# Idle products in w1, a narrower last block of w2, one product for each layer norm sum, and six chunks of V on VectorE in three groups

## The chip, the cores and the metric

The kernel runs on one core of one Trainium2 chip. The metric is the device time of one execution in microseconds (us). Where this text names engines it uses the profile's short names: PE is the matrix engine (TensorE), PEld its weight loads, DVE is VectorE, ACT is ScalarE, POOL is GpSimd, and SP is the engine whose queue issues the loads.

## The reference

One token goes through two identical pairs of layers: an attention with a long cache, and a dense layer with gelu. Everything is float32.

```
D = 512; H, Sk, Dh = 32, 4096, 128; F = 1376
def A(x):                      # 32 heads, one query
    q = (x @ wq) per head
    p = softmax(q . k_cache * Dh**-0.5)
    return (p . v_cache) @ wo
def B(x):
    return gelu(x @ w1 + b1) @ w2 + b2
x = A_x
x = x + A(layernorm(x)); x = x + B(layernorm(x))
x = x + A(layernorm(x)); x = x + B(layernorm(x))
```

The two passes use the same caches and the same weights. K and V are 67 MB each, so the work is nearly all reading.

## The kernel before, in words

The 32 heads are worked in 8 groups of 4. A group's K and its V are one block each of 128 rows by 16384 columns (8.4 MB), cut into C = 8 chunks of NC = 2048 columns. Three homes in one large tile, `arena`, hold blocks in turn (`RING`). A pair of weight blocks (a group's wo and the next group's wq, 2 MB) has a home of its own, `PAIR`. All these loads are issued on SP's one queue, in the order of the program, as soon as the place they write to has been read for the last time. In a steady group SP issues pair, K, V in a row: the pair's home is free once `out_product` of the group before has run, K's and V's homes are free by then too.

A group runs like this. `group` first adds the last partial sums of the group before (`sum_up`, 4 products on PE), then computes the scores of its K (32 products of 8 by 512), then `out_product` of the group before, then the softmax. `partly` works on V: PE takes the first BY_PE = 3 chunks (`values`), and `weighted` lets DVE multiply the other 5 chunks by their weights in place (line 266) and add them up pairwise (line 271). Meanwhile `next_queries` on PE makes the queries of the next group. `sum_up` waits for DVE's last addition.

The first pass goes through groups 0 to 7, the second through 7 to 0; in the second the loop variable `n` counts from 2 to 7, and n = 2 to 6 work as above. Between the passes stands the first `mlp`. It has no spare home: each of its 11 blocks of w2 (512 columns each) is loaded over the four rows of w1, so `load_w2(c)` is issued as soon as the products with row c of w1 have run, and the loads of the next weights and of K (`behind_w2`) are issued as soon as blocks of w2 have been used. At the end, the second `mlp` has w1 and w2 in homes of their own, loaded in pieces far ahead.

`mlp` computes x @ w1 in 4 steps of 4 products (one for each quarter of the F columns, FJ = 344 columns each), and beside it the layer norm's mean and variance: `minus_mean` makes a sum over 128 partitions with four products of 32 columns of weights each. The hidden vector is turned into 32 by 11 blocks, 4 quarters below each other; 11 times 32 is 352, so each quarter is padded by 8 rows on the host. Then come 11 steps of 4 products with w2.

`idle` issues a product of zeros with something that already lies in `arena`; its result is used by nobody. Each float32 product stands as two rows on PE and two on PEld in the profile.

## Time and profile before

| what | value |
|---|---|
| time, median of 3 runs | 673.58 us (673.3 to 674.3) |
| profiled execution, its own time | 673.92 us |
| its span, first to last instruction | 672.1 us |
| mean granted TensorE clock | 0.782 |
| PE, DVE, ACT, POOL busy | 59%, 49%, 3%, 1% |
| moved by the DMA queues | 285.98 MB, 425 GB/s over the span |

The page gives busy times by engine, the span in 40 slices, and the groups of instructions. Busy shares of a whole span mix stages; so the trace is asked by stretch. A releaser behind an arrow is what ended an idle time. "In flight" on the chain of waits, a DMA row, is the time from the issue of a load to its landing, so it holds the time in which the load stood behind others in its queue.

### The profile page before, as it was taken

The page shows a single profiled execution, that of the slowest core. Times are in us where ns is not written, and L with a number is a line of the kernel's source. Part 1 is how long each engine was busy: PE and PEld are TensorE (multiplying, and loading weights), DVE is VectorE, ACT ScalarE, POOL GpSimd, SP SyncE. Part 2 cuts the span into 40 slices and gives each one's busy share as a digit, 9 for nine tenths or more (in the row PEclk, how much of TensorE's full clock was granted, in tenths as well). Part 3 has the DMA queues.
Part 4 walks back from the last instruction along what each step waited for, and adds up shares of the span by engine and source line. Part 5 has one row for each costly group of instructions (what it writes and reads, how often), then busy time and mean ns, then how long its engine had stood idle before and what let it go on. Part 6 is the DMA issues. An engine that isn't in the chain of part 4 may idle for free. (4 is left out here: it accounts for less than half of the span.)

```text
span 672.1 us, 5775 instructions
## 1 busy us (share of the span) xinstructions
PE 397.9 (59%) x2460; PEld 108.2 (16%) x2460; DVE 329.1 (49%) x480; ACT 22.8 (3%) x48; POOL 4.8 (1%) x23
## 2 busy tenths in 40 slices
PE   3442753747617556386777878738526566284685
PEld 1110210211102111121213222101101112021122
DVE  2049186293682845912212221492772936918522
ACT  0010000000000000002000110000000000000000
POOL 1000000000000000000000000000000000000000
PEclk9567775887758757777978999987759767688788
DMA  9999999999999999999999999999999999999996
GB/s 375 437 437 434 437 430 437 410 461 437 437 434 404 462 430 414 433 438 422 435 413 384 432 451 425 427 445 434 430 429 416 458 433 433 434 433 414 433 418 275
DMA packets 11545, 285.98 MB, mean 425 GB/s; under 512 B 1792, under 2 KB 1792, under 8 KB 3584
## 3 DMA queue, kind: packets, MB, share of 16 engines
q1 hardware_dynamic: 11088, 285.61, 98.9%
q8 instruction: 19, 0.31, 0.2%
q10 hardware_dynamic: 432, 0.01, 0.0%
q14 instruction: 6, 0.05, 0.0%
HBM read 285.62 MB, written 0.00 MB: 425 GB/s over the span
## 5 line engine op out<-in xcount | busy, mean ns | idle before, releaser
L111 PE MATMUL pO<-arena,cells 128*128 128x512 f32 (+4 forms) x376 | 93.7, 632 | 147.2 <-DVE arena L271 128.2
L111 PE MATMUL pS<-arena,front 128*8 128x512 f32 x1036 | 145.5, 702 | 36.2 <-DMA arena<-in_k 32.4
L266 DVE TENSOR_TENSOR arena<-arena 128x10240 f32<-128x10240 f32 x11 | 119.1, 10825 | 31.6 <-DMA arena<-in_v 28.2
L111 PE MATMUL pO<-arena 128*4 128x512 f32 x584 | 94.5, 804 | 44.5 <-DMA arena<-in_v 42.7
L271 DVE TENSOR_TENSOR arena<-arena 128x2048 f32<-128x2048 f32 (+1 forms) x33 | 98.5, 2984 | 0.7
L229 DVE TENSOR_REDUCE cells<-pS 128x1 f32<-128x512 f32 x16 | 11.1, 692 | 154.3 <-PE pS L111 154.3
L111 PEld LDWEIGHTS pO<-arena,cells 128*128 128x128 f32 (+3 forms) x376 | 27.9, 122 | 197.3 <-DVE arena L271 137.4
L111 PEld LDWEIGHTS pS<-arena,front 128*8 128x8 f32 x1036 | 31.3, 101 | 157.0 <-issue 116.1
L111 PE MATMUL pS<-arena,cells 128*1 128x128 f32 (+1 forms) x328 | 49.2, 362 | 6.8 <-DMA arena<-in_w 4.6
L281 DVE STREAM_TRANSPOSE arena<-pO 128x512 f32<-128x512 f32 x16 | 11.5, 717 | 55.0 <-PE pO L111 55.0
L243 PE MATMUL pO<-front,arena 128*128 128x128 f32 x64 | 13.1, 339 | 36.6 <-ACT arena L238 36.6
L111 PEld LDWEIGHTS pO<-arena 128*4 128x4 f32 x584 | 16.5, 102 | 108.3 <-issue 103.3
L238 ACT ACTIVATE arena<-pS,cells 128x512 f32<-128x512 f32 x16 | 12.4, 778 | 500.4 <-DVE cells L234 500.4
L170 DVE STREAM_TRANSPOSE arena<-pO 32x128 f32<-32x128 f32 x64 | 19.9, 311 | 18.3 <-PE pO L111 17.3
L111 PEld LDWEIGHTS pS<-arena,cells 128*1 128x1 f32 (+1 forms) x328 | 21.5, 113 | 42.1 <-issue 32.5
L232 DVE TENSOR_REDUCE cells<-cells 128x1 f32<-128x8 f32 x16 | 2.6, 161 | 29.4 <-PE pO L111 29.2
L243 PEld LDWEIGHTS pO<-front,arena 128*128 128x128 f32 x64 | 8.2, 163 | 49.6 <-ACT arena L238 48.4
L170 DVE STREAM_TRANSPOSE arena<-pS 32x128 f32<-32x128 f32 x44 | 13.7, 310 | 0.8
L248 DVE STREAM_TRANSPOSE cells<-cells 128x32 f32<-128x32 f32 x16 | 3.4, 214 | 6.7 <-ACT arena L238 5.5
L172 DVE STREAM_TRANSPOSE arena<-pS 128x128 f32<-128x128 f32 x3 | 0.9, 317 | 10.3 <-PE pS L111 10.3
L383 DVE MEMSET pS<- 128x512 f32 x11 | 5.3, 485 | 1.2
L198 DVE TENSOR_SCALAR cells<-cells,pS 128x4 f32<-128x4 f32 x4 | 0.9, 234 | 9.0 <-PE pS L111 9.0
(63 smaller groups left out, 74.6 us busy)
## 6 DMA issues: line engine op xcount, KB each, us to landing
arena<-in_w SPq DMA_DIRECT2D x13, 2048.0 KB, 11.3
arena<-in_k SPq DMA_DIRECT2D x4, 4096.0 KB, 25.0
arena<-in_v SPq DMA_DIRECT2D x2, 4096.0 KB, 38.8
arena<-in_w SPq DMA_DIRECT2D x6, 1024.0 KB, 20.5
arena<-in_v SPq DMA_DIRECT2D x3, 2048.0 KB, 42.7
arena<-in_v SPq DMA_DIRECT2D x1, 6144.0 KB, 30.3
arena<-in_w SPq DMA_DIRECT2D x6, 688.0 KB, 31.2
arena<-in_v SPq DMA_DIRECT2D x4, 1024.0 KB, 46.5
```

The lines of the kernel that those rows point to most:

```text
L111: tc.keep_in_program_order(nc.tensor.matmul(*a, **kw))
L170: nc.vector.transpose(t[q], src[q, P * j : P * (j + 1)])
L172: nc.vector.transpose(t, src[:, :P])
L229: nc.vector.tensor_reduce(ml[:, 0:1], pS, axis=AX.X, op=ALU.max)
L232: nc.vector.tensor_reduce(m, mt[:, :C], axis=AX.X, op=ALU.max)
L238: nc.scalar.activation(p, pS, AF.Exp, bias=bias[:, 0:1], scale=sc, accum_out=ml[:, 0:1])
L243: tc.keep_in_program_order(nc.tensor.transpose(pT[:, b].rearrange("p j r -> p (j r)"), p[:, P * b : P * (b + 1)], ident))
L248: nc.vector.transpose(lt, ml)
L266: nc.vector.tensor_tensor(t, t, w.unsqueeze(2).to_broadcast([P, 4 * J * (C - BY_PE), P]), op=ALU.mult)
L271: nc.vector.tensor_tensor(a, a, b, op=ALU.add)
L281: nc.vector.transpose(ot, pO)
L383: nc.vector.memset(pS, 0.0)
```

## The change

Four parts.

1. **Idle products in w1.** In the first `mlp` three idle products are put behind the first three steps of w1, of 128, 256 and 256 columns, after that step's `load_w2`. They write columns 128 and up of the PSUM tile `pS`.
2. **w2's last block of 96 rows.** FJ becomes 352 and the four quarters of F are no longer padded each: three have 352 columns and the last has 320 (`FL`). So w2's 11th block has only 96 rows that matter (`PL`), and its load and its products take 96 rows in place of 128. w1's loads keep their size.
3. **Layer norm sums.** `minus_mean` is one product with 128 columns of weights in place of four with 32. It runs twice in each of four layer norms.
4. **Six of V's chunks on DVE.** For n = 3, 4 and 5 of the second pass `by_pe` is 2 in place of 3: PE takes two chunks, DVE six.

```diff
-FJ = F // J
 FB = 11
-W1C = FJ * J
+FJ = 32 * FB
+
+FL = F - 3 * FJ
+PL = 96
...
     def minus_mean(s, at):
-        for j in range(J):
-            matmul(at[32 * j : 32 * j + 32, :], negmean.to_broadcast([P, 32]), s, start=True, stop=True)
+        matmul(at, negmean.to_broadcast([P, P]), s, start=True, stop=True)
         return at
...
-    def weighted(pt, home):
-        first = home + NC * BY_PE
-        t = at(first, NC * (C - BY_PE)).rearrange("p (n d) -> p n d", d=P)
-        w = pt.rearrange("p c j b -> p (c j b)")[:, 4 * J * BY_PE :]
-        nc.vector.tensor_tensor(t, t, w.unsqueeze(2).to_broadcast([P, 4 * J * (C - BY_PE), P]), op=ALU.mult)
-        n = C - BY_PE
+    def weighted(pt, home, by_pe):
+        first = home + NC * by_pe
+        t = at(first, NC * (C - by_pe)).rearrange("p (n d) -> p n d", d=P)
+        w = pt.rearrange("p c j b -> p (c j b)")[:, 4 * J * by_pe :]
+        nc.vector.tensor_tensor(t, t, w.unsqueeze(2).to_broadcast([P, 4 * J * (C - by_pe), P]), op=ALU.mult)
+        n = C - by_pe
...
             for j in range(J):
-                matmul(pO[32 * j : 32 * j + 2, :FJ], pairs(xs)[:, c, :], w1_t[c][:, FJ * j : FJ * (j + 1)],
+                n = FL if j == 3 else FJ
+                matmul(pO[32 * j : 32 * j + 2, :n], pairs(xs)[:, c, :], w1_t[c][:, FJ * j : FJ * j + n],
                        start=(c == 0), stop=(c == 3))
...
             if load_w2:
                 load_w2(c)
+                if c < 3:
+                    idle(pS[:, P:], P if c == 0 else 2 * P)
...
         for c in range(FB):
+            n = PL if c == FB - 1 else P
             for j in range(J):
-                matmul(pS[32 * j : 32 * j + 1, :P], g[:, c : c + 1], w2_t[c][:, P * j : P * (j + 1)],
+                matmul(pS[32 * j : 32 * j + 1, :P], g[:n, c : c + 1], w2_t[c][:n, P * j : P * (j + 1)],
...
     def load_w2(first, a, b):
-        load(first + U * a, w2[:, U * a : U * b])
+        if b < FB:
+            load(first + U * a, w2[:, U * a : U * b])
+        else:
+            assert a == FB - 1
+            tc.keep_in_program_order(nc.sync.dma_start(at(first + U * a, U)[:PL], w2[:PL, U * a :]))
...
-            t = partly(pt, blocks(v, g, v_home, ((0, 6), (6, 8)) if n == 2 else ((0, C),)), v_home)
+            t = partly(pt, blocks(v, g, v_home, ((0, 6), (6, 8)) if n == 2 else ((0, C),)), v_home,
+                       BY_PE - 1 if 2 < n < 6 else BY_PE)
```

On PE, at the first `mlp`, the order before was this (w1's steps write `pO` with 2 by 344, the layer norm's sums write `pS` with 32 by 1; what a row waits for stands behind it):

```order
L111 MATMUL pO<-arena,cells 2x344 [waits DMAHW0_49,DVE_49,Pool_49]
L111 MATMUL pO<-arena,cells 2x344 x3
L111 MATMUL pS<-cells 32x1 x4
L111 MATMUL pO<-arena,cells 2x344 [waits DMAHW1_49]
L111 MATMUL pO<-arena,cells 2x344 x3
L111 MATMUL pS<-cells 32x1 [waits DVE_49]
L111 MATMUL pS<-cells 32x1 x3
L111 MATMUL pO<-arena,cells 2x344 [waits DMAHW2_49]
L111 MATMUL pO<-arena,cells 2x344 x3
L111 MATMUL pO<-arena,cells 2x344 [waits DMAHW3_49]
L111 MATMUL pO<-arena,cells 2x344 x3
```

The same place on PE now, with the idle products (they write `pS` with 128 by 128 and 128 by 256, and read `front`):

```order
L113 MATMUL pO<-arena,cells 2x352 x2
L113 MATMUL pO<-arena,cells 2x320
L113 MATMUL pS<-cells 128x1
L113 MATMUL pS<-arena,front 128x128 [waits DVE_49]
L113 MATMUL pO<-arena,cells 2x352 [waits DMAHW1_49]
L113 MATMUL pO<-arena,cells 2x352 x2
L113 MATMUL pO<-arena,cells 2x320
L113 MATMUL pS<-cells 128x1 [waits DVE_49]
L113 MATMUL pS<-arena,front 128x256 [waits DVE_49]
L113 MATMUL pO<-arena,cells 2x352 [waits DMAHW2_49]
```

Between two steps of w1 there is now an idle product, and the first two of the three wait for DVE: the first for the copy of the mean out of `pS` (line 200 of before), the second for the clearing of the two sums in `pS` (line 207 of before). The next step of w1 stands behind them on PE.

On DVE, a group of the second pass before (lines 266 and 271 are `weighted`, the transposes between them belong to `next_queries`):

```order
L266 TENSOR_TENSOR arena<-arena 128x10240
L271 TENSOR_TENSOR arena<-arena 128x4096
L170 STREAM_TRANSPOSE arena<-pS 32x128
L271 TENSOR_TENSOR arena<-arena 128x2048
L170 STREAM_TRANSPOSE arena<-pS 32x128
```

And in the groups n = 3, 4 and 5 now, where the same functions stand at lines 267 and 272:

```order
L267 TENSOR_TENSOR arena<-arena 128x12288
L272 TENSOR_TENSOR arena<-arena 128x6144
L172 STREAM_TRANSPOSE arena<-pS 32x128
L272 TENSOR_TENSOR arena<-arena 128x2048
L172 STREAM_TRANSPOSE arena<-pS 32x128
```

The multiplication and the first addition are wider by one chunk each; the order around them stays. Everything else keeps its order on every engine, SP's queue included; two of its loads shrink from 128 by 512 to 96 by 512.

## Rows read from the trace of the kernel before

**Rows 1.** The page: engines, DMA share by slices, one queue (packets, MB, share).
```profile
PE 397.9 (59%) x2460; PEld 108.2 (16%) x2460; DVE 329.1 (49%) x480; ACT 22.8 (3%) x48; POOL 4.8 (1%) x23
...
DMA  9999999999999999999999999999999999999996
...
q8 instruction: 19, 0.31, 0.2%
```
**Rows 2.** Stretches: PE, PEld, DVE, ACT, POOL busy; clock, DMA share, GB/s.
```profile
20.00:355.00 335.00, 192.66 (x1012) 49.71 (x1012) 170.14 (x213) 12.46 (x24) 0.10 (x1) 0.74 1.00 430
355.00:375.00 20.00, 15.81 (x228) 6.19 (x232) 4.27 (x28) 0.21 (x1) 2.17 (x8) 0.91 0.99 387
375.00:660.00 285.00, 175.87 (x1070) 47.17 (x1066) 148.20 (x204) 9.96 (x22) 0.30 (x2) 0.80 1.00 432
```
**Rows 3.** Chain of waits, its end: start, us, what.
```profile
650.71 17.53 DMA arena<-in_w
...
668.29 1.06 PE pS L111 x24
```
**Rows 4.** Timeline of PE and DVE, w1's steps in the first mlp.
```profile
355.42 0.76 PE L111 MATMUL pO<-arena,cells 128*2 128x344 f32 x8 [0.69 <-DVE cells L181]
...
356.92 0.76 PE L111 MATMUL pO<-arena,cells 128*2 128x344 f32 x8 [0.70 <-DMA arena<-in_w]
...
358.59 1.32 PE L111 MATMUL pO<-arena,cells 128*2 128x344 f32 x8 [0.88 <-DMA arena<-in_w]
360.26 1.33 PE L111 MATMUL pO<-arena,cells 128*2 128x344 f32 x8 [0.34 <-DMA arena<-in_w]
...
356.49 0.15 DVE L200 COPY cells<-pS 128x1 f32<-128x1 f32 x1
...
358.07 0.06 DVE L207 MEMSET pS<- 128x2 f32 x1
```
**Rows 5.** Stretches of the same place, columns as in rows 2.
```profile
355.00:358.60 3.60, 1.60 (x33) 0.77 (x35) 0.94 (x9) 0.00 (x0) 1.15 (x4) 1.00 1.00 415
358.70:362.00 3.30, 2.96 (x17) 0.60 (x10) 0.32 (x1) 0.00 (x0) 0.00 (x0) 0.50 0.97 361
```
**Rows 6.** DMA issues at 356 us and at the end: KB, us to landing.
```profile
arena<-in_w SPq DMA_DIRECT2D x1, 512.0 KB, 5.2
...
out<-cells SPq DMA_DIRECT2D x1, 2.0 KB, 1.4
```
**Rows 7.** Groups by line and shape, DVE's work on V: busy us, mean ns.
```profile
L266 DVE TENSOR_TENSOR arena<-arena 128x10240 f32<-128x10240 f32 x11 | 119.1, 10825 | 31.6 <-DMA arena<-in_v 28.2 <-issue 3.4
...
L271 DVE TENSOR_TENSOR arena<-arena 128x4096 f32<-128x4096 f32 x11 | 48.7, 4425 | 0.4
```
**Rows 8.** Timeline of PE, sum_up and scores of n = 6; stretches as in rows 2.
```profile
584.89 1.89 PE L111 MATMUL pO<-arena,cells 128*4 128x512 f32 x8 [11.19 <-DVE arena L271]
...
588.73 9.72 PE L111 MATMUL pS<-arena,front 128*8 128x512 f32 x64 [1.95 <-DMA arena<-in_k]
...
590.00:594.00 4.00, 4.00 (x24) 0.83 (x20) 0.00 (x0) 0.00 (x0) 0.00 (x0) 0.50 1.13 492
594.30:602.00 7.70, 7.70 (x48) 2.29 (x40) 0.91 (x2) 0.00 (x0) 0.00 (x0) 1.00 0.98 426
```
**Rows 9.** SP's queue, two issues, and the DMA issue of the first.
```profile
559.04 0.42 SPq L107 DMA_DIRECT2D arena<-in_v  x1
602.12 0.33 SPq L107 DMA_DIRECT2D arena<-in_w  x1
...
arena<-in_v SPq DMA_DIRECT2D x1, 48.9
```
**Rows 10.** Groups by line and shape: layer norm sums, idle products.
```profile
L111 PEld LDWEIGHTS pS<-arena,front 128*128 128x128 f32 x12 | 2.0, 208 | 5.2 <-issue 5.2
...
L111 PEld LDWEIGHTS pS<-cells 128*32 128x32 f32 x64 | 2.0, 122 | 5.0 <-issue 4.0 <-DVE cells L199 1.1
...
L111 PE MATMUL pO<-arena,front 128*128 128x256 f32 x4 | 1.4, 431 | 0.0
```

More of the change, by code (lines that the diff above doesn't have):

```diff
@@ L343, in load_w1 @@
     def load_w1(first, a, b):
-        load(first + W1C * a, w1[:, W1C * a : W1C * b])
+        load(first + F * a, w1[:, F * a : F * b])
     def load_w2(first, a, b):
-        load(first + U * a, w2[:, U * a : U * b])
+        if b < FB:
[3 more added lines that the diff above has]
+            tc.keep_in_program_order(nc.sync.dma_start(at(first + U * a, U)[:PL], w2[:PL, U * a :]))
     def in_rows(first, n, rows):
@@ L404, in group, with partly @@
         return acc, *weights(p)
-    def partly(pt, v_blocks, home):
+    def partly(pt, v_blocks, home, by_pe=BY_PE):
         for c, t in v_blocks:
-            if c < BY_PE:
+            if c < by_pe:
                 values(c, pt, t, c)
-        return weighted(pt, home)
+        return weighted(pt, home, by_pe)
     negm, z, sc, nsc = first_queries(xs, s, wq_t, wide=True)
@@ L465, in behind_w2 @@
             begin_k(SHARED + 2 * NC, 2)
-    own, xb = mlp(x1, s1, in_rows(SHARED, W1C, 4), in_rows(SHARED, U, FB),
+    own, xb = mlp(x1, s1, in_rows(SHARED, F, 4), in_rows(SHARED, U, FB),
                   lambda i: load_w2(SHARED, *W2_AT_CHANGE[i]), behind_w2)
@@ L533, in decode_layers @@
     x1, s1 = set_x(own, 1.0, acc, queries=False)
-    own, xb = mlp(x1, s1, in_rows(A_AT, W1C, 4), in_rows(A_AT + 11 * U, U, FB))
+    own, xb = mlp(x1, s1, in_rows(A_AT, F, 4), in_rows(A_AT + 11 * U, U, FB))
     y = small("y", 4)
@@ L547 @@
         x=A_x, k=A_k_cache, v=A_v_cache, wq=A_wq, wo=A_wo, w1=B_w1, b1=B_b1, w2=B_w2, b2=B_b2).items()}
-    pad = 32 * FB - FJ
-    w2 = np.pad(a["w2"].reshape(J, FJ, D), ((0, 0), (0, pad), (0, 0)))
-    b1 = np.pad(a["b1"].reshape(J, FJ), ((0, 0), (0, pad)))
+    w2 = np.pad(a["w2"], ((0, J * FJ - F), (0, 0)))
+    b1 = np.pad(a["b1"], (0, J * FJ - F))
     wq = columns(a["wq"]).reshape(P, 4, G, J, J, 32)
@@ L563 @@
         w=apart(np.array(w).transpose(0, 2, 1, 3).reshape(2, P, G * NC)),
-        w1=columns(a["w1"]).reshape(P, 4 * J * FJ),
+        w1=columns(a["w1"]).reshape(P, 4 * F),
         b1=b1.reshape(J, FB, 32).transpose(0, 2, 1).reshape(P, FB),
```

## The prediction

> **What bounds the kernel now.** I read the page first. Its DMA line is at 9 in 39 of 40 slices, while no compute engine is busy for more than 59% [rows 1]. The stretches show the rate: 430 GB/s up to 355 us, 432 from 375 to 660, and 387 between 355 and 375 [rows 2]. Those 20 us are the first mlp, the only place in which reading falls behind. At 432 GB/s their bytes would take 20 × 387/432 = 17.9 us, so about 2.1 us are lost there. The chain of waits ends in a load of w2 issued at 650.71 and landed 17.53 us later, and behind it stand only the last 1.06 us of products and some small steps to the end at 672.1 [rows 3]. So three things can shorten this kernel: fewer bytes, less loss between 355 and 375, and a shorter end behind the last load. Work taken off PE or DVE elsewhere is worth nothing by itself; work added there costs nothing until a load is issued too late for its queue.
>
> **Fewer bytes: the 96 rows.** Two loads drop 32 rows of 512 floats: 2 × 32 × 512 × 4 B = 0.131 MB, at 432 GB/s 0.30 us. Both lie where the queue is the limit, one in the mlp between the passes, the other last of all. If the rows are shared out over all 16 engines, each has 6 in place of 8, and 0.30 us is saved. If 8 rows stayed with an engine, 12 engines would do what they did and nothing would be saved. No transfer of 96 rows stands in this trace, so the bounds are 0 and 0.30; I take 0.30. [...] The products with that block take as long as before, since a product's columns are the same.
>
> **The idle products.** Before, the four steps of w1 start at 355.42, 356.92, 358.59 and 360.26; the first two take 0.76 us each, the last two 1.32 and 1.33 [rows 4]. [...] The idle products fill the gaps in which the clock fell. Their price comes from the products of 256 columns, 1.4 us for two, 0.70 each [rows 10]; one of 128 I estimate at half, 0.35. Now step by step. The first may start when line 200 has ended, 356.49 + 0.15 = 356.64 [rows 4], so it ends near 357.05, 0.13 late for step two, which waited for its load until 356.92. The second waits for line 207, 358.07 + 0.06 = 358.13, so it ends near 358.9, and step three starts 0.3 late. At the full clock it ends at 359.66 against 358.59 + 1.32 = 359.91, 0.25 earlier. The third idle product then runs to 360.36, and step four ends at 361.12 against 361.59, 0.47 earlier. Each step's end releases a load of w2, and the turning of the hidden vector, gelu, the steps of w2 and the loads of the next weights and of K follow the last one. So the issues of this stretch come 0.1 later at first and 0.25 to 0.47 earlier afterwards.
>
> How much of that does the DMA take up? A load of 512 KB issued at 356 takes 5.2 us to land [rows 6]; alone it would be 0.524 MB / 432 GB/s = 1.2 us plus about the 1.4 us that the 2 KB of the result take [rows 6]. So on the engine that is last some 2.6 us of other loads still stand ahead of it, while the rate of 387 says that other engines do wait. A gain of 0.47 at the issue is then worth between 0 and 0.47; I take 0.3. SP's queue is only helped: the load of a step is issued by that step's own products, ahead of the idle one.
>
> **The sums of the layer norms.** Eight times four products become one. Before, a sum is 8 rows on PEld of 122 ns, 0.98 us of engine time that largely overlaps PE; now it is 2 rows of about 208 ns (the loads of 128 columns of an idle product), 0.42 [rows 10]. Up to 0.5 us each, then, if PE stood in front of it. It mostly doesn't: in both mlps the steps of w1 wait for loads, at the start the scores wait for K, and only in the layer norm after the first mlp does the sum stand between the new x and the scores. I take 0.05, between 0 and 0.5.
>
> **Six chunks on DVE.** In three groups the multiplication grows from five chunks to six, 10825/5 = 2.17 us more, and the first addition from two chunks to three, 4425/2 = 2.21 more [rows 7]: 4.4 us in each group. PE loses 8 of its 24 short rows, ahead of a load for which it waits anyway. What stands behind DVE: `sum_up`, which waits for DVE's last addition, then the scores, `out_product`, and with its end SP's issue of the next pair, K and V. In the last of the three groups `sum_up` starts at 584.89 and takes 1.89, and the scores wait 1.95 us more for K until 588.73 [rows 8]. So 1.95 of the 4.4 us are covered, and the scores start 2.4 us later, directly behind `sum_up`. They take 9.72 us because the clock is at 0.50 up to 594 and at 1.00 only afterwards [rows 8]: some 5.4 us of them run low, and at the full clock all would take 9.72 − 5.4/2 = 7.0. Starting later and without a gap, less of them should run at the low level; so the issue at 602.12 [rows 9] comes between 1 and 2.4 us later. Is the queue empty by then? The V that was issued at 559.04 lands 48.9 us later, at 607.94 [rows 9], 5.8 us behind the issue of 602.12. Less 1.4 us for a load to get going, 4.4 us are in hand for the engine that is last. So this part costs nothing: the cover is K's and V's loads in the queue. Nor does it gain anything that a row shows.
>
> **The sum.** Bytes 0.30, idle products 0.3, layer norms 0.05, six chunks 0: 0.65 us. The profiled execution took 673.92 us, 1.8 more than its span, and becomes 673.3. It lay 0.34 above the median of the three runs, 673.58; so the median becomes 672.9. A measurement of this kernel can tell about 0.2%, 1.35 us, from no change, so the likeliest outcome counts as no change: 0.58, with its own range from 672.3 to 673.5.
>
> **Rivals.**
>
> *The stretch from 355 to 375 gives back most of its 2.1 us*, since loads issued early help all those behind them. For it speaks that the rate is lowest exactly there; against it that the loads there take 5.2 us to land, so there is a queue on the last engine. With 1.5 us from it and 0.30 from the bytes: 671.8. Chance 0.12.
>
> *One load of instructions less.* Queue q8 brings instructions, 19 packets for 0.2% of 16 engines [rows 1]: 0.002 × 16 × 672.1 / 19 = 1.1 us of one engine each (0.85 to 1.4 with the rounding), on the same engines that carry the data. PE and PEld have 4920 rows [rows 1]. The change takes away 24 products of the layer norms' sums and 12 of V, and adds 3 idle ones: 33 products fewer, of 4 rows each, 132 rows, so 4788 remain; 19 × 132/4920 is half a packet. If one falls away, and from the engine that ends last, the time is 672.9 − 1.1 = 671.8. Against it: it may as well be another engine's. Chance 0.08. [...]
>
> *The idle products come too late for the clock.* Both waits for DVE put them behind the gap that they should fill. If the clock falls at 358.6 all the same, what is left of the second one takes twice as long, step three ends at 360.4, the third takes 1.4, and step four ends at 363.1 in place of 361.6. Then the loads behind come 1.5 us later: 673.3 + 1.5 = 674.8. [...] Chance 0.10.
>
> *Six chunks starve the queue: slower.* In the groups n = 4 to 6 PE sits idle 11.19 us ahead of `sum_up` [rows 8], and will for some 16. If the scores then run at the low clock to the end, they take twice the 7.0 us of the full one, 14.0 against 9.72, and with the later start the issue comes 2.4 + 4.3 = 6.7 us later. Beyond the 4.4 in hand that is 2.3 us in which the last engine has nothing to read; once it has waited, the following groups are late too and have that much more in hand, so it is paid about once. 672.9 + 2.3 = 675.2. It decides from a delay of 4.4 us on. Against it: before, the clock rose during the scores, after PE had worked for a while [rows 8], and now it works without a gap. Chance 0.07.
>
> *Nothing reaches the end*: the 96 rows go over 12 engines and the queue swallows the earlier issues: 673.5. Chance 0.05.
>
> **How the numbers follow.** Faster by over 0.2% (under 672.2): both fast rivals nearly whole, 0.19, and the lower edge of the forecast, 0.02: 0.21. Slower by over 0.2% (over 674.9): most of the last but one, 0.05, and a third of the late idle products, 0.03: 0.08. The rest, 0.71, is no change. The range goes from 671.7, the fast rivals, to 674.5, part way to the late idle products.
>
> **What would show it.** Right: the granted clock stays at 1.00 between 358 and 362; steps three and four of w1 take 0.76 us each and the last ends 0.4 to 0.5 earlier against the landing of its row; the stretch of 355 to 375 moves at some 393 GB/s; the multiplication of 12288 columns takes 13.0 us, the scores of n = 4 to 6 wait for `sum_up` and no longer for K, and the rate from 375 to 660 stays 432. Wrong: a clock of 0.50 in the mlp; a rate well under 430 around 515, 560 or 605 us, or a chain that goes through DVE there; an end behind the last load that is shorter by more than 0.2 us; fewer packets on q8.

## The result, and the profile after

The kernel after takes 674.93 us (median of 22 runs, 673.72 to 677.89), the kernel before 673.52 on the same chip (22 runs, 672.58 to 676.19). The ratio is 1.0017, with a 95% interval from 1.0009 to 1.0025: 0.6 to 1.7 us slower, where 672.9 was forecast with a range from 671.7 to 674.5. The size is about what such a measurement can just tell; the sign is settled. Since the kernel before came out between 673.52 and 674.10 in different comparisons, what follows goes by ratios, each against the runs of before on the same chip. Of 674 us, 0.0010 is 0.67 us, and the interval of one ratio is about 0.0010 to either side.

The profiled execution of after took 677.13 us by its own time, 2.2 above its median, that of before 673.92. So the two profiles lie further apart than the kernels do, and a difference is believed here only where several kernels repeat it.

The page of after: PE's and DVE's busy times, the DMA share by slices, then the queue of the instructions (packets, MB, share).

```profile
PE 392.0 (58%) x2394; PEld 109.0 (16%) x2394; DVE 341.7 (51%) x480; ACT 22.9 (3%) x48; POOL 4.9 (1%) x23
...
DMA  9999999999999999999999999999999999999995
...
q8 instruction: 19, 0.31, 0.2%
```

PE has 66 rows fewer, DVE is busier, and reading is still what fills the span. The whole moves 285.85 MB in place of 285.98, as the 96 rows should make it, and as many packets of instructions come [rows 1].

Stretches of after (us; PE, PEld, DVE, ACT, POOL busy; granted clock, DMA share, GB/s), as in rows 2 and rows 5:

```profile
20.00:355.00 335.00, 190.56 (x1012) 48.66 (x1012) 170.04 (x213) 12.46 (x24) 0.10 (x1) 0.75 1.00 430
355.00:375.00 20.00, 16.39 (x202) 7.02 (x206) 4.19 (x28) 0.21 (x1) 2.17 (x8) 1.00 0.98 369
375.00:660.00 285.00, 170.87 (x1054) 46.61 (x1046) 161.02 (x204) 9.97 (x22) 0.31 (x2) 0.80 1.00 431
355.00:358.60 3.60, 2.58 (x22) 1.14 (x22) 0.83 (x9) 0.00 (x0) 0.67 (x4) 1.00 1.01 417
358.70:362.00 3.30, 3.30 (x22) 1.08 (x22) 0.51 (x1) 0.00 (x0) 0.42 (x1) 1.00 0.97 361
```

Ahead of the first mlp nothing changed. The stretch of the mlp reads 369 GB/s where before read 387 [rows 2]: 20 × (387 − 369)/432 = 0.8 us more lost. This happens although the idle products do what they are for: from 358.7 to 362 the clock is 1.00, where it was 0.50 [rows 5]. Behind the mlp the rate is 431 in place of 432; over 285 us one unit is 0.66 us, so in these two profiles some of the loss may lie there too.

The timeline of after, PE and two rows of DVE, in the first mlp and the layer norm behind it, up to the scores:

```profile
355.32 0.77 PE L113 MATMUL pO<-arena,cells 128*2 128x352 f32 x8 [0.69 <-DVE cells L183]
356.02 0.38 PE L113 MATMUL pS<-cells 128*128 128x1 f32 x2
356.79 0.49 PE L113 MATMUL pS<-arena,front 128*128 128x128 f32 x2 [0.39 <-DVE cells L201]
357.21 0.77 PE L113 MATMUL pO<-arena,cells 128*2 128x352 f32 x8
357.91 0.38 PE L113 MATMUL pS<-cells 128*128 128x1 f32 x2
358.67 0.70 PE L113 MATMUL pS<-arena,front 128*128 128x256 f32 x2 [0.39 <-DVE pS L208]
359.30 0.77 PE L113 MATMUL pO<-arena,cells 128*2 128x352 f32 x8
360.00 0.70 PE L113 MATMUL pS<-arena,front 128*128 128x256 f32 x2
360.63 0.77 PE L113 MATMUL pO<-arena,cells 128*2 128x352 f32 x8
...
356.58 0.15 DVE L201 COPY cells<-pS 128x1 f32<-128x1 f32 x1
...
358.56 0.06 DVE L208 MEMSET pS<- 128x2 f32 x1
...
369.77 0.62 PE L113 MATMUL pO<-arena,cells 128*2 128x128 f32 x16
370.32 0.38 PE L113 MATMUL pS<-cells 128*128 128x1 f32 x2
370.63 0.62 PE L113 MATMUL pO<-arena,cells 128*2 128x128 f32 x16
371.24 0.38 PE L113 MATMUL pS<-cells 128*128 128x1 f32 x2
372.07 7.05 PE L113 MATMUL pS<-arena,front 128*8 128x512 f32 x64 [0.45 <-DVE pS L208]
```

The steps of w1 take 0.77 us each. But steps two, three and four start 1.89, 3.98 and 5.31 us behind step one; before it was 1.50, 3.17 and 4.84 [rows 4]. No step waits for its load any more: each of the three stands behind an idle product, and the idle products ahead of steps two and three waited 0.39 us each for DVE. Step four ends 6.08 us behind step one's start; before, with its two slow steps, it was 6.17. So of the 0.47 us that were expected 0.09 came. And the single product of a layer norm's sum is a row of 0.38 us on PE, on the path between the queries and the scores too (2.30 us from 369.77 to 372.07).

Two groups of after, DVE's wider steps (busy us, mean ns of one):

```profile
L267 DVE TENSOR_TENSOR arena<-arena 128x12288 f32<-128x12288 f32 x3 | 38.9, 12958 | 6.0 <-DMA arena<-in_v 4.9 <-issue 1.1
...
L272 DVE TENSOR_TENSOR arena<-arena 128x6144 f32<-128x6144 f32 x3 | 19.7, 6558 | 0.1
```

The timeline of PE in n = 6 of after, `sum_up` and the scores, as in rows 8:

```profile
590.94 1.89 PE L113 MATMUL pO<-arena,cells 128*4 128x512 f32 x8 [14.50 <-DVE arena L272]
592.61 8.19 PE L113 MATMUL pS<-arena,front 128*8 128x512 f32 x64
```

The scores stand directly behind `sum_up`, wait for no K, and take 8.19 us in place of 9.72. The chain of waits of the page now goes through DVE in these groups (9% of the span, 1% before), which the prediction had put down as a sign of trouble. That it was none is read from b_six and a_nosix below.

The end of the chain of waits of after, as in rows 3:

```profile
648.78 20.77 DMA arena<-in_w
669.55 0.04 issue
669.60 2.85 PE pS L113 x56
```

In this execution 56 rows of products stood behind the last load in place of 24, and took 2.85 us (1.06 before); the granted clock was 1.00 up to 670 us and 0.50 from there to 672. That may be a part of what sets this execution 2.2 us above the median.

### The profile page after: what moved, and what is told of

It is laid out like the page before. It is cut to its first block, busy times and chain, and to the rows that moved or that the text cites. A ratio compares the mean times of both kernels' runs of the same rounds, so it can differ in the third digit from the quotient of the medians.

```text
span 675.3 us, 5643 instructions
## 1 busy us (share of the span) xinstructions
PE 392.0 (58%) x2394; PEld 109.0 (16%) x2394; DVE 341.7 (51%) x480; ACT 22.9 (3%) x48; POOL 4.9 (1%) x23
## 2 busy tenths in 40 slices
DMA packets 11481, 285.85 MB, mean 423 GB/s; under 512 B 1792, under 2 KB 1792, under 8 KB 3520
## 5 line engine op out<-in xcount | busy, mean ns | idle before, releaser
L113 PE MATMUL pO<-arena,cells 128*128 128x512 f32 (+5 forms) x376 | 91.5, 600 | 156.4 <-DVE arena L272 138.4
L113 PE MATMUL pS<-arena,front 128*8 128x512 f32 (+1 forms) x1042 | 144.3, 688 | 31.0 <-DMA arena<-in_k 26.5
L267 DVE TENSOR_TENSOR arena<-arena 128x10240 f32<-128x10240 f32 (+1 forms) x11 | 125.5, 11407 | 29.5 <-DMA arena<-in_v 28.4
L113 PE MATMUL pO<-arena 128*4 128x512 f32 x560 | 90.4, 801 | 42.7 <-DMA arena<-in_v 40.7
L272 DVE TENSOR_TENSOR arena<-arena 128x2048 f32<-128x2048 f32 (+2 forms) x33 | 104.9, 3179 | 0.7
L113 PE MATMUL pS<-arena,cells 128*1 128x128 f32 (+2 forms) x328 | 51.5, 387 | 13.8 <-DMA arena<-in_w 11.2
L113 PEld LDWEIGHTS pS<-arena,front 128*8 128x8 f32 (+1 forms) x1042 | 31.7, 101 | 148.8 <-issue 114.1
L244 PE MATMUL pO<-front,arena 128*128 128x128 f32 x64 | 11.7, 311 | 36.6 <-ACT arena L239 36.6
L113 PEld LDWEIGHTS pS<-arena,cells 128*1 128x1 f32 (+2 forms) x328 | 22.7, 119 | 51.4 <-issue 40.6
```

Of the source, the lines that this page charges most:

```text
L113: tc.keep_in_program_order(nc.tensor.matmul(*a, **kw))
L244: tc.keep_in_program_order(nc.tensor.transpose(pT[:, b].rearrange("p j r -> p (j r)"), p[:, P * b : P * (b + 1)], ident))
L267: nc.vector.tensor_tensor(t, t, w.unsqueeze(2).to_broadcast([P, 4 * J * (C - by_pe), P]), op=ALU.mult)
L272: nc.vector.tensor_tensor(a, a, b, op=ALU.add)
```

## The experiments

Eighteen kernels were run, in five groups. At first three theories stood against each other. M: the loss is made in the first mlp, by the idle products' waits for DVE and by the longer sums. S: six chunks on VectorE delay the issues so far that the queue runs dry. E: the last block of w2 costs time at the end. Later ones are named where they come up. Each ratio is against before on the same chip; after itself was timed in one such comparison only.

Three columns of this table are read from each kernel's profile: the end of w1's step four behind step one's start, the time from the first query behind the mlp to the first scores, and the rate from 355 to 375 us. "Idle" means how the idle products in w1 stand, "sum" how many products a layer norm's sum has in w1 and behind the mlp.

| kernel | idle | sum | ratio to before | 95% | step four | query to scores | GB/s |
|---|---|---|---|---|---|---|---|
| before | none | 4, 4 | 1 | | 6.17 | 1.97 | 387 |
| after | waits | 1, 1 | 1.0017 | 1.0009 to 1.0025 | 6.08 | 2.30 | 369 |
| b_idle | waits | 4, 4 | 0.9998 | 0.9989 to 1.0008 | 5.66 | 1.97 | 401 |
| b_ln | none | 1, 1 | 0.9991 | 0.9982 to 1.0001 | 5.60 | 2.30 | 398 |
| b_six | none | 4, 4 | 0.9993 | 0.9984 to 1.0002 | 5.59 | 1.98 | 398 |
| b_r96 | none | 4, 4 | 1.0003 | 0.9993 to 1.0013 | 5.65 | 1.97 | 393 |
| a_noidle | none | 1, 1 | 1.0021 | 1.0012 to 1.0031 | 5.80 | 2.29 | 380 |
| a_noln | waits | 4, 4 | 1.0010 | 0.9995 to 1.0025 | 5.71 | 1.98 | 377 |
| a_nosix | waits | 1, 1 | 1.0015 | 1.0006 to 1.0024 | 6.07 | 2.30 | 370 |
| a_r128 | waits | 1, 1 | 1.0015 | 1.0005 to 1.0025 | 6.07 | 2.30 | 376 |
| a_pad33 | waits | 1, 1 | 1.0017 | 1.0005 to 1.0028 | 6.36 | 2.30 | 368 |
| b_pad31 | none | 4, 4 | 1.0010 | 0.9999 to 1.0021 | 6.61 | 1.97 | 355 |
| b_ln_r96 | none | 1, 1 | 1.0006 | 0.9995 to 1.0017 | 5.45 | 2.30 | 392 |
| a_endidle | waits | 1, 1 | 1.0019 | 1.0007 to 1.0031 | 6.07 | 3.48 | 352 |
| a_free | no wait | 1, 1 | 0.9991 | 0.9982 to 1.0001 | 5.59 | 2.29 | 395 |
| a_ln4 | waits | 1, 4 | 1.0004 | 0.9995 to 1.0013 | 6.07 | 1.98 | 370 |
| a_free_ln4 | no wait | 1, 4 | 0.9992 | 0.9983 to 1.0001 | 5.61 | 1.97 | 376 |
| b_delay | none | 4, 4 | 1.0019 | 1.0009 to 1.0030 | 6.16 | 1.97 | 367 |
| best | no wait | 4, 4 | 1.0002 | 0.9993 to 1.0011 | 5.60 | 1.97 | 401 |
| b_seven | none | 4, 4 | 1.0108 | 1.0090 to 1.0125 | 5.50 | 1.97 | 388 |

The profiles agree on where the time goes. By its own time a profiled execution took 672.4 to 673.9 us in the seven kernels whose last column is 392 or more, and 674.1 to 677.1 in the eleven with 380 or less; before, with 387, took 673.92 (b_seven, which loses its time elsewhere, is left out). But this is the loss of single executions: a_free_ln4's profile is among the eleven, with 376 and 674.76 us, while its ratio is 0.9992.

### One part alone

Four kernels are before with one part of the change each.

**b_idle**, the idle products alone:

```diff
             if load_w2:
                 load_w2(c)
+                if c < 3:
+                    idle(pS[:, P:], P if c == 0 else 2 * P)
```

> The kernel before with the three idle products in w1 alone. Theory M (the loss is made in the first mlp: the idle products wait for VectorE, and the next step of w1 stands behind them): 0.2 to 0.5 us slower than before (ratio 1.0003 to 1.0008), 355 to 375 us under 387 GB/s, step three of w1 starting 0.4 to 0.7 later than in before against step one. Theory S (the loss is made by the six chunks, whose late issues let the queue run dry): no slower than before, 0 to 0.4 faster. The prediction on record said 0.3 faster. All three expect the clock at 1.00 through the mlp and w1's steps of 0.76 us.

**b_ln**, the layer norms' sums by one product:

```diff
-        for j in range(J):
-            matmul(at[32 * j : 32 * j + 32, :], negmean.to_broadcast([P, 32]), s, start=True, stop=True)
+        matmul(at, negmean.to_broadcast([P, P]), s, start=True, stop=True)
```

> The kernel before with one product of 128 columns for each layer norm sum alone. Theory M: 0.2 to 0.4 us slower than before (1.0003 to 1.0006), since a product takes 0.38 us where the four took 0.22 and two of them stand between the new x and the scores behind the first mlp; from the first query to the scores some 2.3 us in place of 2.0. Theory S and the prediction on record: within 0.1 us of before.

**b_six**, six chunks on VectorE for n = 3, 4 and 5:

```diff
-            t = partly(pt, blocks(v, g, v_home, ((0, 6), (6, 8)) if n == 2 else ((0, C),)), v_home)
+            t = partly(pt, blocks(v, g, v_home, ((0, 6), (6, 8)) if n == 2 else ((0, C),)), v_home,
+                       BY_PE - 1 if 2 < n < 6 else BY_PE)
```

> The kernel before with six chunks of V on VectorE for n = 3, 4 and 5 alone. Theory S: 0.7 to 1.3 us slower than before (1.0010 to 1.0019); the issues behind out_product come 2 to 4 us later than in before, and the rate falls under 430 GB/s near 520 us, where the first engines to end have nothing to read for about 1 us. Theory M and the prediction on record: within 0.2 us of before (0.9997 to 1.0003), since the engine that is last still has over 2 us in hand.

**b_r96**, the 96 rows, with the split of F into 352, 352, 352 and 320 columns:

```diff
-FJ = F // J
+FJ = 32 * FB
...
+            n = PL if c == FB - 1 else P
```

> The kernel before with the 96 rows of w2's last block alone (and the split of F into 352, 352, 352 and 320 columns that goes with it). Theories M and S and the prediction on record: 0.3 us faster than before (0.9996), the 96-row load taking part on all 16 engines. A third theory, E (the loss is made at the end, where the chain behind the last landing took 2.26 us in the profile of after and 1.40 in that of before): 0.4 to 1.0 us slower, with more than 24 rows of w2's products behind the last landing.

None of the four is measurably slower, and theories M, S and E each forecast a loss for one of them. The loss of after (0.0009 at least) lies outside the intervals of b_idle, b_ln and b_six, so it is none of these parts' alone; that of b_r96 reaches 1.0013, and a_r128 below decides there. (The 0.2 to 0.5 us that M gave b_idle still lie inside its interval.) The timelines tell more than the times. First b_six, whose code in the mlp is that of before; PE, w1's four steps:

```profile
355.23 0.76 PE L111 MATMUL pO<-arena,cells 128*2 128x344 f32 x8 [0.69 <-DVE cells L181]
...
356.73 0.76 PE L111 MATMUL pO<-arena,cells 128*2 128x344 f32 x8 [0.71 <-DMA arena<-in_w]
...
358.41 0.76 PE L111 MATMUL pO<-arena,cells 128*2 128x344 f32 x8 [0.89 <-DMA arena<-in_w]
360.06 0.76 PE L111 MATMUL pO<-arena,cells 128*2 128x344 f32 x8 [0.89 <-DMA arena<-in_w]
```

Without any idle product the clock stayed up here, and step four ends 5.59 us behind step one's start. The 1.32 and 1.33 us of before [rows 4] are thus what happens in some executions only. Of the nine profiles of kernels without idle products, four (b_six, b_ln, b_ln_r96, b_pad31) show all four steps at 0.76 or 0.77 us; in the other five step four takes from 0.81 to 1.33. In all eleven with idle products every step takes 0.76 or 0.77. The row also shows the cover: steps two to four wait 0.71, 0.89 and 0.89 us for their loads, and work put in front of them costs nothing up to that.

The same place in b_idle, with the sums in four products, and the copy on DVE:

```profile
355.22 0.76 PE L111 MATMUL pO<-arena,cells 128*2 128x344 f32 x8 [0.69 <-DVE cells L181]
355.79 0.22 PE L111 MATMUL pS<-cells 128*32 128x1 f32 x8
356.49 0.49 PE L111 MATMUL pS<-arena,front 128*128 128x128 f32 x2 [0.47 <-DVE cells L200]
356.90 0.76 PE L111 MATMUL pO<-arena,cells 128*2 128x344 f32 x8
...
360.12 0.76 PE L111 MATMUL pO<-arena,cells 128*2 128x344 f32 x8
...
356.28 0.15 DVE L200 COPY cells<-pS 128x1 f32<-128x1 f32 x1
```

Here step four ends at 5.66, 0.07 later than in b_six: the waiting idle products use up the cover and no more. With the single sums in front of them, as in after, it is 6.08. The single product is 0.16 us longer on PE (0.38 against 0.22), and the copy of the mean, on which the idle product waits, starts 1.26 us behind step one's start in place of 1.06 (b_idle: 356.28, for a step at 355.22). Twice some 0.2 us beyond a cover that was just used up: on this path each part alone is nearly free, both together cost 0.4 us. This is theory MM, which the next experiments test: idle products and single sums together delay the steps of w1.

### The change without one part

**a_noidle, a_noln, a_nosix and a_r128** are after with one part undone: no idle products, four products for each sum, five chunks everywhere, and 128 rows in w2's last block (the 352 columns stay). The first three take back the diffs above; the last is:

```diff
-            n = PL if c == FB - 1 else P
+            n = P
...
-        if b < FB:
-            load(first + U * a, w2[:, U * a : U * b])
...
+        load(first + U * a, w2[:, U * a : U * b])
```

> After without the three idle products. None of the four parts alone made the kernel slower, so what costs 1.4 us is a sum of two of them. Theory MM (idle products and the wider layer norm products delay the same steps of w1, the last one ends 0.5 us later than with either alone): 1.0 to 1.4 us faster than after, so 673.5 to 673.9, step four of w1 starting 4.85 us behind step one in place of 5.3. Theory S (six chunks, with the loads of the mlp already late): as slow as after, 674.6 to 675.1. Theory F (where the loads of instructions fall, which the number of rows on TensorE shifts): 12 rows fewer move them little, so as slow as after.

> After with the layer norms' sums by four products again. Theory MM: 673.3 to 673.8, 1.1 to 1.6 faster than after; from the first query behind the mlp to the scores 2.0 us in place of 2.3. Theory S: as slow as after. Theory F: 96 rows more on TensorE put the loads of instructions back to about where they are in before, so as fast as before, 673.5; the sixteenth of them then comes near 570 us and not at 597.

> After with five chunks on VectorE in all groups. Theory S (a queue that runs dry near 520 us): as fast as before, 673.5 to 673.9. Theories MM and F: as slow as after, 674.6 to 675.1, since the mlp and, but for 12 rows, the instructions are those of after.

> After with w2's last block loaded and multiplied with all 128 rows. Theories MM, S and F: 0 to 0.3 us slower than after, 674.9 to 675.2. Theory E (the last block of 96 rows costs time at both ends of mlp): 673.5 to 674.2.

Five chunks or 128 rows change nothing that can be measured, so theories S and E fall: a_nosix and a_r128 are as slow as after. With four products for the sums step four ends at 5.71, as MM has it; the time, 1.0010, lies between, but its interval (0.9995 to 1.0025) holds both no gain and the whole loss, and MM had asked for 1.1 to 1.6 us. And a_noidle is a plain miss for MM: without the idle products it stays at 1.0021. Its profile offers a reason, not a proof: its step four runs low in part (1.01 us), and the idle product of 512 columns behind it, which takes 1.12 in after, takes 2.08. Taken out, the idle products would save their waits and lose the clock (0.91 in the mean of 355 to 375 us, 1.00 in after). Against this reason speaks b_r96, whose profile shows the same (0.91 and 2.08 us) at a ratio of 1.0003. The six chunks may have a part as well: a_noidle with five chunks is b_ln_r96 below, at 1.0006; the two intervals overlap.

### The instructions, and the clock at the end

A theory F was left: the change removes 66 rows of products from PE and as many of PEld, so the loads of instructions fall at other moments: the sixteenth packet on q8 starts at 574.6 us in the trace of before and at 597.6 in that of after. (Theory L, in the same expectations, lays the loss to the single sums together with the 352 columns.) **a_pad33** is after with 33 tiny products at an early place where PE waits, **b_pad31** is before with 31. These are 124 rows more, after has 132 fewer, and the 256 between them are about one packet's worth by an estimate from rows 1 (4920 rows for 19 packets, some 259 each); so by F the later packets of b_pad31 should come about where after has them:

```diff
     negm, z, sc, nsc = first_queries(xs, s, wq_t, wide=True)
+    for _ in range(33):
+        matmul(pK[0][:, :1], negmean.to_broadcast([P, P]), one, start=True, stop=True)
```

> After with 33 tiny products (128 columns of weights, 1 column of data, into a free PSUM tile) behind the first queries, where TensorE waits for the first K: 132 rows more on PE and PEld, as many as the change takes away, and no other work. Theory F (the loads of instructions fall at worse moments because the change removes rows): back to 673.4 to 673.9, and the last loads of instructions come near 648 and 666 us as in before. Theory L (the wider product of the layer norm's sums costs time itself, together with the 352 columns): as slow as after, 674.6 to 675.1.

> [...] Theory F: 674.4 to 675.0, the last load of instructions near 669. Theory L: as before, 673.5 to 673.9.

a_pad33 has 2460 rows on PE again and is as slow as after, which speaks against F, though not cleanly. b_pad31 is unclear: 1.0010, between nothing and 1.4 us. Its page has 20 packets on q8 in place of 19, each 1.1 us of one engine by the prediction's working and 0.98 in the mean of this trace, and that would fit as well. The traces show one thing more. In both padded kernels a packet of instructions starts at 359 us, where the other eighteen have one near 350 and one near 366; and step four of w1, which waits for its load in both, starts 5.59 and 5.85 us behind step one, against 4.68 to 4.84 in the eleven others that wait there. So the pads brought a delay of their own into the mlp. A cleaner case against F is a_free below: its packets in the mlp come at 350, 366, 375 and 388 us, those of after at 350, 367, 376 and 390, and it is not slow.

**b_ln_r96** has two of the four parts, the single sums and the 96 rows; it has as many PE rows as b_ln.

> Two parts of the change, the layer norm's single products and the 96 rows with their 352 columns; five chunks, no idle products. It has as many rows on TensorE as the layer norm part alone, which was no slower than before. Theory F: 673.2 to 673.9. Theory L: 674.5 to 675.0, since all four slow kernels so far have both the single products and the 352 columns.

It came out at 1.0006, which is neither, and its interval (0.9995 to 1.0017) leaves both theories open. It is a_free, below, that speaks against L: it has both of these parts and is not slow.

**a_endidle** is after with idle products in the last mlp too:

```diff
         idle(pS)
+        if not load_w2:
+            idle(pK[0], U // 2)
...
+            elif c in (3, 7):
+                idle(pK[0], U // 2 if c == 3 else P)
```

> After with idle products in the last mlp as well (256 columns behind the last step of w1, 256 behind w2's fourth step, 128 behind its eighth, into a free PSUM tile). Theory C (in some executions the clock falls to 0.50 in w2's last steps, which then take up to 1 us longer; in the profile of after they did, in that of before not): 0.4 to 0.9 us faster than after, clock 1.00 behind 669 us. Theories F and L: as slow as after, 674.6 to 675.2.

The clock stayed at 1.00 in all stretches from 664 to 672 us of its profile, the products behind w2's last load took 0.84 us for 24 rows, and the kernel is as slow as after. Nothing speaks for theory C, by which the low clock that the profile of after shows at the end sets the medians apart; the interval still admits the least gain that it forecast, 0.4 us.

### The delays taken out

What the slow variants of after share, a_noidle apart, is a step four at 6.07 or later. **a_free** keeps the idle products and takes away what they wait for. They no longer write columns of `pS`, which DVE reads and clears, but add zeros (2 columns of zero weights) into the sums of w1's first quarter, which are open in `pO` at that moment:

```diff
-                    idle(pS[:, P:], P if c == 0 else 2 * P)
+                    n = P if c == 0 else 2 * P
+                    matmul(pO[:2, :n], zero[:, :2], at(C_AT, n), start=False, stop=False)
```

> After with idle products that wait for nobody: as many columns, but with 2 columns of zero weights and added into the open sums of w1's first quarter. Theory MM, as the traces have it now: the loss is made between step one of w1 and the first scores behind the mlp, of pieces: 0.45 us because idle products and the single layer norm products together put step four's end at 6.07 us behind step one's start, in place of 5.6 with either alone; 0.33 us because of the single products between the queries and the scores, 2.30 in place of 1.97; the rest where w2's steps wait for loads that came late. Expected: step four ends 5.6 to 5.7 us behind step one's start, the clock stays at 1.00, 0.4 to 0.8 us faster than after, so 674.1 to 674.5. Theory T (the loss does not lie there but in the second pass): the same step times, but as slow as after.

PE's timeline of a_free at w1's steps:

```profile
355.99 0.38 PE L113 MATMUL pS<-cells 128*128 128x1 f32 x2
356.31 0.38 PE L113 MATMUL pO<-arena,front 128*2 128x128 f32 x2
356.78 0.77 PE L113 MATMUL pO<-arena,cells 128*2 128x352 f32 x8
...
359.06 0.59 PE L113 MATMUL pO<-arena,front 128*2 128x256 f32 x2
360.12 0.77 PE L113 MATMUL pO<-arena,cells 128*2 128x352 f32 x8 [0.46 <-DMA arena<-in_w]
```

The idle products stand directly behind the sums, and step four waits for its load again, 0.46 us. It ends at 5.59, the stretch reads 395 GB/s with the clock at 1.00, and the kernel comes out at 0.9991: some 1.7 us faster than after (1.0017 less 0.9991, 0.0026; the two intervals don't touch), twice what MM forecast. Theory T, by which the loss lies in the second pass, falls. The new idle products are also 0.11 us shorter each, 0.33 in all; that alone would not reach step four, which now waits 0.46 us for its load. So with the other parts in place the loss hangs on how the idle products are built, and what the edit takes away on the timeline are their waits. That much is shown. The size is not explained, since step four moved by 0.49 us only, and neither is a_noidle, which has no such waits and is slow.

**a_ln4** is after with four products for the sums behind the first mlp alone, **a_free_ln4** has both edits:

```diff
+        if four:
+            for j in range(J):
+                matmul(at[32 * j : 32 * j + 32, :], negmean.to_broadcast([P, 32]), s, start=True, stop=True)
+            return at
         matmul(at, negmean.to_broadcast([P, P]), s, start=True, stop=True)
```

> After with four products for each sum in the one layer norm behind the first mlp, single products elsewhere. Theory MM: 1.97 us in place of 2.30 from the first query to the scores, and 0.3 us faster than after, 674.5. Theory T: as slow as after.

> After with both of these. Theory MM: 15.1 to 15.7 us from step one of w1 to the first scores (16.75 in after), 390 to 400 GB/s between 355 and 375 us (369 in after), 673.4 to 674.0, as before or faster. Theory T: 674.6 or more.

a_ln4, PE between the first query and the scores:

```profile
369.27 0.62 PE L113 MATMUL pO<-arena,cells 128*2 128x128 f32 x16
...
371.25 2.33 PE L113 MATMUL pS<-arena,front 128*8 128x512 f32 x20 [0.48 <-DVE pS L212]
```

That is 1.98 us from 369.27 to 371.25, where all kernels with single sums there but one have 2.29 or 2.30 (a_endidle, with a granted clock of 0.90 in the mean of 355 to 375 us, 3.48). The time, 1.0004, is 0.9 us under after; 0.3 was expected, and the intervals overlap a little (up to 1.0013 here, from 1.0009 there), so the size is unsettled. With step four at 6.07 and 370 GB/s as in after, this kernel also speaks against a late step four setting the time by itself. On top of a_free the same edit brings nothing that can be measured (0.9992), and the stretch of that profile reads 376 GB/s where 390 to 400 was expected; the rate of a single profile is a rough witness.

**b_delay** measures what a known delay costs: before with two more idle products of 512 columns ahead of the queries.

```diff
                     idle(pO, U if c == 4 else U // 2)
+                if c == FB - 1:
+                    idle(pO)
+                    idle(pO)
```

> The kernel before with two more idle products of 512 columns behind w2's last step in the first mlp, some 2.2 us of TensorE ahead of the queries, with no other change: what a known delay there costs. If every delay in this stretch reaches the end whole: 2.0 to 2.3 us slower, 675.6 to 675.9. If the queue swallows the first part, as the prediction on record took it (0.3 of 0.47): 1.4 us slower. If it swallows all that the last engine has in hand: under 0.7 us.

```profile
366.76 0.70 PE L111 MATMUL pO<-arena,front 128*128 128x256 f32 x2
...
368.21 2.41 PE L111 MATMUL pO<-arena,front 128*128 128x256 f32 x6
```

In PE's timeline of b_delay the idle products ahead of the queries take 2.41 us, where one takes 0.70: the delay is 1.71 us, not the 2.2 that were expected. (The row groups all six of its rows under the first one's columns; the two new products have 512.) The ratio of 1.0019 is 1.3 us, 0.6 to 2.0. So some three quarters of a delay here reach the end, with an interval from a third to all of it; the prediction had taken 0.3 of 0.47, which is 0.64. The delay stands ahead of the queries, not in w1's steps, where the prediction's stood.

### How much cover the chunks have, and what is left of the change

**b_seven** is b_six with seven chunks on VectorE in the same three groups:

```diff
-                       BY_PE - 1 if 2 < n < 6 else BY_PE)
+                       BY_PE - 2 if 2 < n < 6 else BY_PE)
```

**best** is what is left when the delays are out: the 96 rows and the idle products of a_free, four products for each sum, five chunks.

> The kernel before with seven chunks on VectorE for n = 3, 4 and 5: VectorE's work in a group from 19.8 us to 28.3 (24.1 with six), so that the issue behind out_product comes 5 to 7 us later than in before. By the prediction's figure, 4.4 us in hand for the last engine: 1 to 2.5 us slower, with the chain through VectorE and a rate under 425 GB/s near 520 us. If nothing of that reaches the end: within 0.3 us of before, as six chunks.

> The 96 rows and the idle products that wait for nobody, with four products for each layer norm sum and five chunks throughout: what is left of the change when the delays are taken out. Theory MM: 15.0 to 15.8 us from step one of w1 to the first scores, 390 to 402 GB/s between 355 and 375 us, 0.3 to 0.9 us faster than before (0.9987 to 0.9996), as a_free and a_free_ln4. If the single products gained something elsewhere, it would be slower than a_free_ln4 by that.

Stretches of b_seven (columns as above), one for each group from n = 4 on:

```profile
500.00:540.00 40.00, 21.00 (x100) 5.91 (x100) 28.87 (x28) 0.87 (x2) 0.00 (x0) 0.80 0.95 403
540.00:585.00 45.00, 21.73 (x100) 6.29 (x100) 34.78 (x30) 0.87 (x2) 0.00 (x0) 0.69 0.98 417
585.00:630.00 45.00, 21.35 (x116) 5.80 (x116) 33.54 (x30) 0.87 (x2) 0.00 (x0) 0.77 0.94 399
```

And rows of its timeline in the last of these groups, DVE's multiplication, `sum_up`, and the issues of the pair in the group before and in this one:

```profile
568.71 15.09 DVE L266 TENSOR_TENSOR arena<-arena 128x14336 f32<-128x14336 f32 x1
...
597.64 1.89 PE L111 MATMUL pO<-arena,cells 128*4 128x512 f32 x8 [17.46 <-DVE arena L271]
...
565.40 0.33 SPq L107 DMA_DIRECT2D arena<-in_w  x1
...
611.94 0.33 SPq L107 DMA_DIRECT2D arena<-in_w  x1
```

b_seven is 1.0108: 7.3 us slower, where 1 to 2.5 were expected. Against 432 GB/s the three stretches lose 40 × 29/432 = 2.7, 45 × 15/432 = 1.6 and 45 × 33/432 = 3.4 us, 7.7 in all. Six chunks cost nothing, seven cost some 2.4 us in each group. From one issue of a pair to the next 46.5 us pass (565.40 to 611.94); the 18.9 MB of a pair, a K and a V take 43.7 at 432 GB/s.

best is 1.0002, the same as before, where 0.3 to 0.9 us faster was expected. No kernel here beats before by more than the measurement can tell; a_free and a_free_ln4 come nearest (0.9991 and 0.9992, with intervals that end at 1.0001).

## Why the prediction was wrong

The sum gave 0.65 us to be gained; 1.1 us were lost. The prediction's call of no change within 0.2% covers 0.0017, but its range did not.

**The bound** was read rightly. The loss lies for the greater part in the stretch from 355 to 375 us that the prediction named as the one weak place: there after reads 369 GB/s, before 387 and a_free 395, while from 375 to 660 us it is 431, 432 and 432.

**The idle products: the failing step.** The term was 0.3 us of gain, from step four ending 0.47 us earlier. The prediction put the first idle product at 356.64, step two 0.13 late, step three first 0.3 late and then ahead, and step four 0.47 ahead. Alone, in b_idle, it goes nearly so: step two 0.18 late, step three 0.41 late, step four's end at 5.66 in place of the 5.70 that follow from the prediction. In after it is 0.39 late, 0.81 late and 0.09 ahead, and in place of a gain of 0.3 us the idle products as built cost some 1.7 against ones that wait for nobody (a_free). (The first idle product was priced at half of 0.70, 0.35 us; it takes 0.49.) What failed is that the idle products and the single sums were costed apart: the times of DVE's copy and clearing, 356.49 and 358.07 [rows 4], were taken from before, while the change itself moves both, by the single sums on which DVE waits. The prediction weighed exactly that the idle products wait for DVE, and used the wait of the old sums. In the prediction's sum this is the error: each of its four terms was worked out on the kernel before, and two of them meet in the same gaps.

**The clock** was taken for a constant. The 0.50 of rows 5, at which the last two steps take 1.32 and 1.33 us [rows 4], is one execution's. Where it does not fall, the four steps end at 5.59 without idle products (b_six), and these have nothing to give back: b_idle is no faster than before. The rival of idle products that come too late for the clock has the wrong mechanism with nearly the right time: 674.8 was its price, 674.93 came, at a clock of 1.00. That is luck. The nine profiles without idle products differ among themselves, four with all steps at 0.76 or 0.77 us and five with a slower step four, though each is of another kernel. That the clock differs between executions of one kernel shows in the mean granted clock: 0.776 to 0.794 in the 17 runs of before beside best.

**The sums of the layer norms: wrong sign.** 0.05 us were to be gained, up to 0.5, from eight rows of 122 ns on PEld against two of 208 [rows 10]. On PE's timeline the four narrow products are a row of 0.22 us and the wide one is 0.38 (0.24 and 0.38 at the variance behind the mlp). Busy time of the weight loads was summed where the row of the whole step was there to be read. On PEld's timeline the eight narrow loads of a sum in before are two rows of 0.13 us (the second stands here), four loads of 122 ns mean in each, so they lie beside each other; the two wide ones of after are one row of 0.30:

```profile
356.00 0.13 PEld L111 LDWEIGHTS pS<-cells 128*32 128x32 f32 x4 [0.16 <-issue]
...
356.02 0.30 PEld L113 LDWEIGHTS pS<-cells 128*128 128x128 f32 x2 [0.59 <-issue]
```

The cost is 0.33 us between the first query and the scores, and the push that overdraws the cover of w1's steps. Why four narrow products take less on PE than the wide one, 0.22 us against 0.38, these rows do not show.

**Six chunks: right, and just so.** The multiplication takes 12.96 us where 13.0 was forecast, the scores stand behind `sum_up`, and b_six (0.9993) and a_nosix (1.0015, with after at 1.0017) put the price at nothing that can be measured. The 4.4 us in hand fit b_seven as well: its seventh chunk is 4.3 us more of DVE's work in a group, and 2.4 of them are lost, so by this estimate the six chunks had left some 1.9. But the rival's "paid about once" was wrong: b_seven pays in each of its three groups, where the 46.5 us from issue to issue are longer than the loads take.

**The 96 rows.** The bytes went (0.13 MB), the time can't be told: b_r96 is at 1.0003 where 0.9996 was forecast, within its interval. b_ln_r96 against b_ln (1.0006 and 0.9991) and best against before speak rather against a gain. So no run shows the 0.30 us of the sum. The rows say nothing on how many engines share such a load. The products with this block take as long as the others, as the prediction had it: a row on PE is 272 ns in the mean with 96 rows and 272 with 128, in the first mlp of after.

**How the delays reach the end** is in keeping with b_delay: three quarters there, between a third and all, where 0.64 was taken.

**What stays open.** Step four's 0.49 us and the queries' 0.33 are 0.8 us at the scores, and by b_delay 0.6 at the end, of the 1.1 us (0.6 to 1.7) to be explained. The profile of after shows more in between (w2's steps wait twice 0.47 us for loads), but a_pad33, as slow, does not. a_ln4 has the late step four and came out at 1.0004. And a_noidle stays slow without a wait; that the falling clock takes the place of the waits there was read from one profile and not tried, and b_r96 has the same clock, 0.91 in the mean of 355 to 375 us, without the loss.

## What to carry to other kernels

When two edits stand in the same gap, work out the gap once with both in it: each fitted alone under a cover of 0.7 to 0.9 us, and together they overdrew it. Filler work should wait for nobody, so let it write where no other engine reads or clears; here that was worth some 1.7 us of the changed kernel, and nothing measurable against the kernel before. A clock level read from one profile is one execution's, and is worth a second profile before a gain is built on it.

## What the runs showed of the hardware

A single product of 128 columns of weights and one column of data takes 0.38 us on PE's timeline at a granted clock of 1.00; four products of 32 columns with the same data take 0.22. Four loads of 32 columns of weights, 122 ns each in the mean, lie in a row of 0.13 us. One more chunk on VectorE in three groups cost nothing that can be measured (b_six 0.9993), and the next one 7.3 us (b_seven 1.0108). Thirty-three tiny products at a place where PE waits cost nothing that can be measured (a_pad33 1.0017, after 1.0017). In the two kernels in which a packet of instructions, 0.96 and 0.98 us long, came while w1's last row was loading, the step that waits for this row started 0.7 to 1.2 us later than in the others; that the packet is the reason was not tried.
